# Recurrence: r and k scaled one step further ahead, behind the masking; step 21's logits products behind its bonus products

## The chip, the cores and the metric

One core of one Trainium2 chip. The metric is the device time of one execution in microseconds (us). TensorE is PE in the rows (PEld is its loading of weights), VectorE DVE, ScalarE ACT, GpSimd POOL, SyncE SP. SP only issues DMAs here.

## The reference

Three stages: a linear recurrence with a bonus term, a top-1 mixture of experts, and a second one with soft slots. The change touches the first stage alone.

```python
def _attn_ref(r, k, v, w, u):            # r, k, v: [B=4, H=8, S=768, D=48]
    for t in range(S):
        kt, vt, rt = (k[:, :, t], v[:, :, t], r[:, :, t])
        cur = np.einsum('bhd,bhe->bhde', u[None] * kt, vt)
        y[:, :, t] = np.einsum('bhd,bhde->bhe', rt, state + cur)
        state = w[None, :, :, None] * state + np.einsum('bhd,bhe->bhde', kt, vt)

x = y.transpose(0, 2, 1, 3).reshape(B * S, H * D)      # 3072 x 384
# first mixture, for rows with x @ w_skip > 0:  e = argmax(x @ w_gate)
#     x += prob[e] * relu(x @ w1[e]) @ w2[e]             8 experts, F = 1024
# second mixture: logits = x @ phi (32 slots), softmax over rows gives the slots' inputs,
#     each expert runs its 4 slots, softmax over slots combines them -> out 3072 x 384
```

## The kernel before

**The recurrence in steps.** The sequence is cut into 6 chunks of 128 and there are 4 batches: 24 steps, step j being chunk c = j // 4 of batch b = j % 4 with all 8 heads. Inside a chunk the recurrence is a masked product (like attention without a softmax): r and k are scaled by powers of the decay w, `sc` = k.r, masked below the diagonal, the bonus (u.k.r) put on the diagonal, and the result multiplied with v; what came before the chunk enters through a state `sp`.

**The order** is that of the program: the schedule is manual, each engine executes its instructions as the loop over i writes them. A step i is software-pipelined:

- `load(i+3)` (L510): SP issues the DMA of r and k (`rkb`, L514) and of k and v (`kvt`, L519). A DMA into a buffer waits until the last reader of what lay in it is done; SP issues in order, so what is behind a waiting DMA waits too.
- `scores(i)` (L646): PE makes `sc` (L656) from the scaled `rks` of step i; ACT copies the two blocks that need no mask (`later`, L710); then PE does step i-1's products of r with the state (`inter`, L734) and the first half of its products with v (`av(i-1, 0)`, L753). Then comes a call `between()`, and behind it the bonus products (L666), from `pd` = r*k into the PSUM tile `ud`, which ACT copies to `dts` (L668).
- `trx(i-2)` transposes y of step i-2 (L764, ACT L765).
- `prep(i+1)` (L630): DVE multiplies r and k of step i+1 with decay powers (L635, L636) into `rks`, one of three buffers; POOL makes `pd` (L638). `prepk` makes `kt` on POOL (L644).
- `upd(i)` (L679, PE), `bonus(i)` (L682, PE transposes `dts` back), `moved(i)` (ACT L695), `av(i-1, 1)` (PE, second half, then ACT copies y, L758).
- `past(i)` (L705, DVE) multiplies `sc` with the mask into `at`. The PSUM tile `sc` has one buffer, so `sc` of step i+1 on PE waits for `past(i)`.
- `amask(i)` (L714, DVE) writes the diagonal of `at` from the transposed bonus; `av(i, 0)` on PE waits for it.

**The routing of the first mixture** is threaded through the same steps, per chunk: `route1` (L828: the logits products `lgt`, L837 on PE, copied by ACT, L838) in the steps with i % 4 == 2, and in `between` of steps 21 and 23 for the last groups; `route2` (PE transposes `lgs`, L865), `route2b` (L876, small DVE operations L882 to L901), `route3` (PE), `gates`, `places` and `count` (DVE), `route4` (L952: POOL L956, DVE L957, L958) and `hots` (L798, DVE or POOL). `gathered` (L804) are PE products of these lists. `stored` (L809) writes four finished tiles of x to DRAM in steps 9, 13, 17, ...; `wload` (L963) starts the loads of the first experts' weights in steps 20 to 22, behind the loads of the recurrence.

**Behind the recurrence** come the rest of the routing, the gather of the experts' rows (L1197 on POOL) and the two mixtures.

The change touches `NRK` (number of `rkb` buffers), `load`, `prep` and the loop.

Of the kernel before, what the change touches and what calls it, by code (L numbers as in the profile page):

```python
# [8 lines left out]
F32 = mybir.dt.float32  # L9
# [10 lines left out]
P = 128  # L20
NC_ = S // P
NT = B * NC_
DM = H * D
# [7 lines left out]
PR = 112  # L31
# [443 lines left out]
def tile_main(ctx, tc, rk, kv, wu, wcat, phi, w1, w2, v1, v2, r_in, k_in, v_in, w_in, u_in, wcn, out, dbg=None, force=False):  # L475
    nc = tc.nc
# [8 lines left out]
    wk = ap.enter_context(tc.tile_pool(name="wk", bufs=2))  # L485
# [4 lines left out]
    PE_, DVE_, ACT_, POOL_, SP_ = (mybir.EngineType.PE, mybir.EngineType.DVE, mybir.EngineType.Activation, mybir.EngineType.Pool, mybir.EngineType.SP)  # L490
    mst = ExitStack()
    mst.enter_context(tc.manual_schedule(engines={PE_, DVE_, ACT_, POOL_, SP_}))
    NRK = 5
    ones = fp.tile([P, P], BF16, name="ones")
    nc.vector.memset(ones, float(E))

    def warm(n, w=P):

        wp = ps.tile([P, 2, 4 * P], F32, tag="y", name="wp")[:, 0, 0 : 4 * w]
        for _ in range(n):  # L500
            nc.tensor.matmul(wp, ones, ones[:, 0:w].rearrange("p (o n) -> p o n", o=1).to_broadcast([P, 4, w]), start=True, stop=True)  # L501
# [6 lines left out]
    T = {}  # L508

    def load(j, first=True, last=True):  # L510
        c, b = divmod(j, B)
        if first:
            t = T[j] = {"rk": rkb[j % NRK]}
            nc.sync.dma_start(out=t["rk"], in_=rk[c, b])  # L514
        if not last:
            return
        t = T[j]
        t["kv"] = wk.tile([P, 2, DM], F32, tag="kvt", bufs=5, name=f"kvt{j}")
        nc.sync.dma_start(out=t["kv"], in_=kv[c, b])  # L519

    load(0, last=False)
# [81 lines left out]
    prt = psc.tile([PR, 4, P], F32, name="prt")  # L603
    nc.vector.tensor_mul(prt, pt[:, :, 0:P], iw.to_broadcast([PR, 4, P]))
    pkt = prt[:, :, ::-1]
# [21 lines left out]

    yts = {}

    def prep(j):  # L630
        t = T[j]
        rkt = t["rk"]
        rks = wk.tile([PR, 2, 4, P], F32, tag="rks", bufs=3, name=f"rks{j}")
        t["rs"], t["ks"] = rks[:, 0], rks[:, 1]
        nc.vector.tensor_mul(rks[:, 0], rkt[:, 0], prt)  # L635
        nc.vector.tensor_mul(rks[:, 1], rkt[:, 1], pkt)  # L636
        t["pd"] = wk.tile([PR, 4, P], F32, tag="pd", name=f"pd{j}")
        nc.gpsimd.tensor_mul(t["pd"], rkt[:, 0], rkt[:, 1])  # L638

# [63 lines left out]
    def past(j):  # L703
        t = T[j]
        nc.vector.tensor_mul(t["at"][:, :, 0:4], t["sc"][:, :, 0:4], mh.rearrange("s (a o t) -> s a o t", a=1, o=1).to_broadcast([P, 2, 4, HT]))  # L705
# [122 lines left out]
    def route1(g, pool=ps, tag="r"):  # L828
        c, (j0, nb) = g, GR[g]
        r = RT[c] = {}  # L830
        lgt = pool.tile([P, nb * P], F32, tag=tag, name=f"lgt{c}")
        r["lgs"] = ry.tile([P, nb * P], F32, tag="lgs", bufs=2, name=f"lgs{c}")
        yt, b0 = yts[j0 // B], j0 % B
        for q in range(2):
            for s2 in range(2):
                p = 2 * s2 + q
                nc.tensor.matmul(lgt[64 * s2 : 64 * s2 + 64, :], wcs[:, p, :], yt[:, p, b0 : b0 + nb, :].rearrange("d b t -> d (b t)"), start=(q == 0), stop=(q == 1))  # L837
        nc.scalar.copy(r["lgs"], lgt)  # L838
# [184 lines left out]
    if True:  # L1023
        for i in range(NT):
            if i + 3 < NT:
                load(i + 3)
            rc, rb = divmod(i - 5, B)
            rok = 0 <= rc < NC_ - 1
            if i == 0:
                decays()  # L1030
                warm(5, 48)
                prep(0)
                prepk(0)
                for hf in range(2):
                    r0 = 64 * hf
                    nc.vector.tensor_copy(usel[r0 : r0 + D, :, hf : hf + 1], wt[r0 : r0 + D, 1, :].rearrange("p (a o) -> p a o", o=1))
            scores(i, lambda: route1(i // 2 - 6) if i in (21, 23) else None)
            if i > 1:
                trx(i - 2)
            if rok and rb == 3 or i == 22:  # L1040
                route3(rc, place=T[i]["rp"])
            if rok and rb == 2 and rc < 4:
                route2(rc)
            if i == 21:
                route2(4)
            if i == 23:
                route2(5)
            if rok and rb == 1 and rc < 4:
                route1(rc)
            if i == 0:  # L1050
                prep(1)
                prepk(1)
                for ts in spf:
                    for t in ts:
                        nc.gpsimd.memset(t[:, 4 * D :], 0.0)
            elif i + 1 < NT:
                prep(i + 1)
                prepk(i + 1)
            if i > 0:
                state(i - 1)  # L1060
            upd(i)
            if i == 22:
                c4pt = ps.tile([P, P], F32, tag="r", name="c4pt")
                nc.tensor.transpose(c4pt, c4t.rearrange("p q s -> p (q s)"), ident)
            bonus(i)
            moved(i)
            if i > 0:
                av(i - 1, 1)
            if i in (13, 17, 21, 22):
                gathered(len(LI))  # L1070
            past(i)
            if i == 22:
                nc.vector.tensor_reduce(mcs[:, 0:1], c4pt, axis=AX.X, op=ALU.max)
                dgt = rt.tile([32, 32], F32, tag="dg", bufs=1, name="dgt")
                nc.vector.tensor_scalar(dgt, ident[0:32, 0:32], mcs[0:32, 0:1], None, op0=ALU.mult)
                amask(22)
                weave("pgpgg", g=gates(4), p=places(4))
                tokens(4, nc.gpsimd)
                hots(4, range(4), nc.gpsimd)
            decayed(i)  # L1080
            if i == 21:
                nc.vector.tensor_reduce(cmax, cmg.rearrange("t g s -> t s g"), axis=AX.X, op=ALU.max)
                c4t = fourfold(nc, "t", rt, cmax)
                amask(21)
                route2b(4)
            elif rb == 0 and 1 <= rc < 4:
                route4(rc - 1)
            if i % B and 9 <= i < 22:
                hots(i // B - 2, (i % B,) if i < 20 else (2, 3), nc.vector if i < 20 else nc.gpsimd)
            if i not in (21, 22):  # L1090
                amask(i)
            if rok and rb == 2 and rc < 4:
                route2b(rc)
            if rok and rb == 3:
                weave("gpgpg", g=gates(rc), p=places(rc))
                count(rc)
                tokens(rc, nc.gpsimd)
                hots(rc, (0,) if rc < 3 else (0, 1), nc.vector if rc < 3 else nc.gpsimd)
                if rc == 3:
                    route4(3)  # L1100
            if i == 8:
                wok = rt.tile([PR, 2, 4], F32, tag="wok", bufs=1, name="wok")
                nc.vector.tensor_scalar(wok[:, 0], wt[:, 0, :], WLO, None, op0=ALU.is_ge)
                nc.vector.tensor_scalar(wok[:, 1], wt[:, 0, :], WHI, None, op0=ALU.is_le)
                wmn = mk.tile([PR, 1], BF16, name="wmn")
                nc.vector.tensor_reduce(wmn, wok, axis=AX.XY, op=ALU.min)
            if 20 <= i < 23:
                wload(i - 20)
            if i % B == 1 and 9 <= i < 25:
                stored(i - 9, B)  # L1110
            if i == 22:
                stored(16, B)
            if 3 <= i < 7:
                constants(i)
            if i == 4:
                odd = rt.tile([P, NT], F32, tag="odd", bufs=1, name="odd")
                nc.vector.tensor_reduce(odd[:, 0:1], ident.rearrange("p (a r) -> p r a", r=2)[:, 1:2], axis=AX.X, op=ALU.add)
                nc.vector.tensor_scalar(odd[:, 1:2], odd[:, 0:1], float(-NT), None, op0=ALU.mult)
                tf = rt.tile([P, 2, NT], F32, tag="tf", bufs=1, name="tf")
                nc.scalar.copy(tf, tj_i)  # L1120
                nc.vector.tensor_scalar(tj[:, 0], tf[:, 0], float(NT), odd[:, 1:2], op0=ALU.mult, op1=ALU.add)
                nc.vector.tensor_sub(tj[:, 1], tf[:, 1], tj[:, 0])
                nc.gpsimd.iota(ipl.bitcast(I32), pattern=[[E, CAP]], base=-NOROW, channel_multiplier=0)
                nc.gpsimd.tensor_copy(ipl, ipl.bitcast(I32))
                for t in tok:
                    nc.gpsimd.memset(t, 0.0)
            if i == 6:
                sf = rt.tile([P, E], F32, tag="sf", bufs=1, name="sf")
                nc.vector.tensor_reduce(sf, ident.rearrange("p (q r s) -> p s q r", q=4, s=E)[:, :, :, 0:2], axis=AX.XY, op=ALU.add)
                nc.scalar.copy(selb, sf)  # L1130
# [224 lines left out]
    if True:  # L1355
# [4 lines left out]
        for n in range(NS + 1):  # L1360
# [12 lines left out]
            f = e - 1  # L1373
# [300 lines left out]
```

## Time and profile before

| | us |
|---|---|
| median of 3 runs | 350.14 |
| lowest and highest run | 348.92, 354.14 |
| the profiled execution | 348.07 |
| its span, first to last instruction | 346.3 |
| outside the span | 1.77 |

The profile is of one execution. The span falls into a start (to 8 us), the recurrence (8 to 125), the rest of the routing (125 to 140), the first mixture (140 to 299) and the second (299 to 346). Busy time is time in which an engine executes; "issue" in a row means that an engine stood idle and waited for nothing that the profile shows; PEclk is the clock that TensorE was granted, as a share of full speed.

### The profile page before, as it was taken

The numbers are of one execution on the slowest core, as the hardware profiler recorded it, in microseconds if no ns is written. First come the engines' busy times: TensorE is split into PE (matmuls) and PEld (weight loads), VectorE is DVE, ScalarE is ACT, GpSimd is POOL, SyncE is SP. The second block draws the span as 40 slices with busy tenths as digits, with TensorE's granted clock in tenths as the row PEclk, the third lists the DMA queues.
The fourth block names the chain that finished last, engine by engine and source line by source line (L and its number), as shares of the span: only waits on it lengthen the run. The fifth ranks groups of instructions, "written<-read, shape, count | busy, mean of one in ns | idle before, by whom it ended". The sixth has DMA issues, their size and how long they took to land.

```text
span 346.3 us, 10440 instructions
## 1 busy us (share of the span) xinstructions
PE 321.4 (93%) x4326; PEld 263.9 (76%) x4326; DVE 226.1 (65%) x510; ACT 159.5 (46%) x353; POOL 139.8 (40%) x181
## 2 busy tenths in 40 slices
PE   8699998999998999999999999999999999999950
PEld 8477776767775782999999999998999998534540
DVE  6637676896969865776675848575676845226850
ACT  3235454444543463554645546464645543121360
POOL 3939685776844544804324232525224002200000
PEclk9969999999999998999999999999999999899995
DMA  7976667684879944899788787878866749779096
GB/s 233 287 220 190 187 189 255 199 269 141 279 191 310 387 163 158 266 310 315 252 288 303 239 281 255 263 257 296 294 197 215 254 124 377 256 268 324 10 338 210
DMA packets 45735, 85.29 MB, mean 246 GB/s; under 512 B 3838, under 2 KB 26672, under 8 KB 45680
## 3 DMA queue, kind: packets, MB, share of 16 engines
q1 hardware_dynamic: 43024, 80.63, 70.8%
q0 software_dynamic: 2128, 3.74, 3.9%
q8 instruction: 36, 0.59, 0.7%
q10 hardware_dynamic: 528, 0.16, 0.2%
q14 instruction: 19, 0.16, 0.1%
HBM read 74.49 MB, written 10.10 MB: 244 GB/s over the span
## 4 chain that ended last, share of the span: by engine, by line
PE 79%; DVE 12%; issue 3%; ACT 2%; POOL 1%; ACTq 0%; DVEq 0%
PE yp L1291 7%; PE yp L1292 6%; PE yp L1293 6%; PE hp L1266 6%; PE hp L1269 6%; PE hp L1267 6%; PE yp L753 4%; PE ehp L216 4%; PE sc L656 3%; PE lgt L837 3%; PE ud L679 3%; PE trp L764 3%; PE yp L734 2%; PE wp L501 2%; PE ud L666 2%
## 5 line engine op out<-in xcount | busy, mean ns | idle before, releaser
L1266 PE MATMUL hp<-xhl,wa 128*128 128x240 f32 x192 | 46.1, 282 | 0.2 <-issue 0.2
L1291 PE MATMUL yp<-wb,hh 128*128 128x384 f32 x128 | 45.2, 353 | 0.0
L1004 DVE TENSOR_TENSOR wa<-w,wa 128x768 fp32r<-128x768 f32 x32 | 30.5, 955 | 22.4 <-ACT wa L1016 22.3
L1267 PE MATMUL hp<-xhl,wa 128*128 128x240 f32 x192 | 44.6, 275 | 0.0
L1292 PE MATMUL yp<-wb,hh 128*128 128x384 f32 x128 | 43.0, 336 | 0.0
L1293 PE MATMUL yp<-wb,hl 128*128 128x384 f32 x128 | 42.9, 335 | 0.0
L1197 POOL DMA_INDIRECT xg<-x_d,idg x16 | 19.9, 1242 | 51.9 <-DVE x L1299 38.1
L638 POOL TENSOR_TENSOR pd<-rkb 112x512 f32<-112x512 f32 x24 | 31.1, 1295 | 18.6 <-PE ud L666 15.3
L1321 POOL DMA_INDIRECT lt_d<-lsr,ids x16 | 17.7, 1106 | 50.2 <-ACT xhl L1256 28.3
L1266 PEld LDWEIGHTS hp<-xhl,wa 128*128 128x128 f32 x192 | 36.2, 189 | 0.5 <-ACT dsbv L135 0.5
L1267 PEld LDWEIGHTS hp<-xhl,wa 128*128 128x128 f32 x192 | 36.2, 189 | 0.0
L714 DVE COPY_PREDICATED at<-ih,ud 128x512 f32<-128x512 int32 x24 | 17.7, 738 | 26.0 <-ACT us L695 16.5
L1004 DVE TENSOR_TENSOR wb<-w,wb 128x768 fp32r<-128x768 f32 x32 | 30.5, 953 | 2.1 <-ACT wb L1016 1.7
L1016 ACT CAST wb<-w 128x768 fp32r<-128x768 f32 x32 | 26.8, 838 | 9.5 <-PE yp L1293 5.5
L753 PE MATMUL yp<-at,kvt 64*48 64x64 f32 (+3 forms) x800 | 27.7, 250 | 1.0 <-DVE at L714 0.4
L1276 ACT ACTIVATE hh<-hp 128x480 fp32r<-128x480 f32 x32 | 18.3, 572 | 22.2 <-PE hp L1269 20.0
L1277 DVE SCALAR_TENSOR_TENSOR hl<-hp,hh 128x480 fp32r<-128x480 f32 x32 | 20.9, 654 | 9.7 <-ACT hh L1276 9.2
L1016 ACT CAST wa<-w 128x768 fp32r<-128x768 f32 x32 | 26.9, 840 | 0.0
L1291 PEld LDWEIGHTS yp<-wb,hh 128*128 128x128 f32 x128 | 24.0, 188 | 3.6 <-issue 3.5
L1269 PE MATMUL hp<-xhl,wa 128*128 128x240 f32 x192 | 26.7, 275 | 0.0
L656 PE MATMUL sc<-rks 48*64 48x128 f32 (+1 forms) x768 | 22.1, 252 | 4.5 <-DVE at L705 2.3
L753 PEld LDWEIGHTS yp<-at,kvt 64*48 64x48 f32 (+1 forms) x800 | 22.2, 125 | 5.3 <-issue 1.6
(346 smaller groups left out, 697.1 us busy)
## 6 DMA issues: line engine op xcount, KB each, us to landing
w<-in_w_dram SPq DMA_DIRECT2D x32, 768.0 KB
v<-in_v_dram SPq DMA_DIRECT2D x29, 768.0 KB
rkb<-in_rk_dram SPq DMA_DIRECT2D x24, 448.0 KB
kvt<-in_kv_dram SPq DMA_DIRECT2D x24, 384.0 KB
x_d<-x SPq DMA_DIRECT2D x5, 768.0 KB
out_dram<-ob SPq DMA_DIRECT2D x5, 768.0 KB
x<-in_v_dram SPq DMA_DIRECT2D x2, 768.0 KB
x_d<-x SPq DMA_DIRECT2D x2, 384.0 KB
```

The costliest lines, as they stand in the source:

```text
L638: nc.gpsimd.tensor_mul(t["pd"], rkt[:, 0], rkt[:, 1])
L656: nc.tensor.matmul(sc[c0 : c0 + HT, g, blocks(p, z), :], ks[r0 : r0 + D, p, HT * z : HT * z + HT], rs[r0 : r0 + D, p, HT * z :], start=Tru ...
L753: nc.tensor.matmul(d, kvt[s0 : s0 + HT, 1, h * D : h * D + m], w, start=(c == ph == z == 0), stop=(ph == z == 1))
L1004: nc.vector.tensor_sub(lv, sl, hv.bitcast(F32))
L1016: nc.scalar.copy(hv, sl)
L1266: nc.tensor.matmul(hp[:, f, 0:ROOM], hi[:, k, fs], xh[:, k, 0:ROOM], start=(k == 0 and f == 0), stop=False)
L1267: nc.tensor.matmul(hp[:, f, 0:ROOM], lo[:, k, fs], xh[:, k, 0:ROOM], start=False, stop=False)
L1269: nc.tensor.matmul(hp[:, f, 0:ROOM], hi[:, k, fs], xl[:, k, 0:ROOM], start=False, stop=(k == 2 and f == 1))
L1277: nc.vector.scalar_tensor_tensor(l, p, 0.0, h.bitcast(F32), op0=ALU.max, op1=ALU.subtract)
L1291: nc.tensor.matmul(YP[e][bl], hh[:, f, bs], hi[:, f, :], start=st, stop=False)
L1292: nc.tensor.matmul(YP[e][bl], hh[:, f, bs], lo[:, f, :], start=False, stop=False)
L1293: nc.tensor.matmul(YP[e][bl], hlo[:, f, bs], hi[:, f, :], start=False, stop=en)
```

## The change

Five edits: `NRK` 5 to 4; `kvt` 5 to 4 buffers; `rks` 3 to 4 buffers; the two scalings leave `prep` for a function `scaled(j)` of their own, which step i calls for j = i+2 behind `past(i)` (up to step 2 behind `amask(i)`; `scaled(0)` and `scaled(1)` stand in step 0); and `route1(4)` of step 21 leaves `between` for a place behind `scores(21)`, which ends with the bonus products. Since `load(j)` reuses the buffer of step j-4 instead of j-5, `rkb` of step j now waits for the scaling and `pd` of step j-4, and `kvt` of step j for `av(j-4, 1)`.

```diff
-    NRK = 5
+    NRK = 4
...
-        t["kv"] = wk.tile([P, 2, DM], F32, tag="kvt", bufs=5, name=f"kvt{j}")
+        t["kv"] = wk.tile([P, 2, DM], F32, tag="kvt", bufs=4, name=f"kvt{j}")
...
+    def scaled(j):
+        if j >= NT:
+            return
+        t = T[j]
+        rkt = t["rk"]
+        rks = wk.tile([PR, 2, 4, P], F32, tag="rks", bufs=4, name=f"rks{j}")
+        t["rs"], t["ks"] = rks[:, 0], rks[:, 1]
+        nc.vector.tensor_mul(rks[:, 0], rkt[:, 0], prt)
+        nc.vector.tensor_mul(rks[:, 1], rkt[:, 1], pkt)
+
     def prep(j):
         t = T[j]
         rkt = t["rk"]
-        rks = wk.tile([PR, 2, 4, P], F32, tag="rks", bufs=3, name=f"rks{j}")
-        t["rs"], t["ks"] = rks[:, 0], rks[:, 1]
-        nc.vector.tensor_mul(rks[:, 0], rkt[:, 0], prt)
-        nc.vector.tensor_mul(rks[:, 1], rkt[:, 1], pkt)
...
+                scaled(0)
                 prep(0)
...
-            scores(i, lambda: route1(i // 2 - 6) if i in (21, 23) else None)
+            scores(i, lambda: route1(5) if i == 23 else None)
+            if i == 21:
+                route1(4)
...
             if i == 0:
+                scaled(1)
                 prep(1)
...
             past(i)
+            if i > 2:
+                scaled(i + 2)
...
                 amask(i)
+            if i <= 2:
+                scaled(i + 2)
```

What stands on the engines, in the order of the program. Names end in the step's or group's number and a number of the tile; lines behind L627 are six higher in the changed kernel.

DVE in step 8, from the last routing operation of chunk 0 (`oh0`) on, before:

```order
L901 SCALAR_TENSOR_TENSOR oh0_923<-lgp0_873,m20_921 128x32
L635 TENSOR_TENSOR rks9_983<-rkb4_133,prt_212 112x512
L636 TENSOR_TENSOR rks9_983<-rkb4_133,prt_212 112x512
L705 TENSOR_TENSOR at8_945<-sc8_928,mh_192 128x2x256
L714 COPY_PREDICATED at8_945<-ih_193,ud8_964 128x2x256
L925 TENSOR_REDUCE lgp0_873<-ex0_918 128x4
L936 TENSOR_TENSOR r20_1016<-ud8_964,oh0_923 128x32
```

and with the change:

```order
L907 SCALAR_TENSOR_TENSOR oh0_925<-lgp0_875,m20_923 128x32
L711 TENSOR_TENSOR at8_947<-sc8_930,mh_191 128x2x256
L637 TENSOR_TENSOR rks10_1011<-rkb2_131,prt_211 112x512
L638 TENSOR_TENSOR rks10_1011<-rkb2_131,prt_211 112x512
L720 COPY_PREDICATED at8_947<-ih_192,ud8_966 128x2x256
L931 TENSOR_REDUCE lgp0_875<-ex0_920 128x4
L942 TENSOR_TENSOR r20_1018<-ud8_966,oh0_925 128x32
```

The masking of step 8 (`at8` from `sc8`) now stands ahead of two scalings, and these are of step 10 instead of step 9. Between the masking and the diagonal (`at8` from `ud8`) stand the two scalings.

PE in step 21, from the end of `av(20, 0)` on, before:

```order
L753 MATMUL yp20_2222<-at20_2128,kvt20_1817 48x64 x4
L837 MATMUL lgt4_2239<-yt4_1895,wcs_140 64x512 x4
L666 MATMUL ud21_2246<-pd21_2169,usel_142 32x128 x4
L764 MATMUL trp19_2253<-ident_149,yt4_1895 128x112 x4
L865 MATMUL lgp4_2259<-ident_149,lgs4_2240 128x128 x4
L682 MATMUL ud21_2246<-ident_149,dts21_2251 128x128
```

and with the change:

```order
L759 MATMUL yp20_2224<-at20_2130,kvt20_1819 48x64 x4
L672 MATMUL ud21_2241<-pd21_2168,usel_141 32x128 x4
L843 MATMUL lgt4_2248<-yt4_1894,wcs_139 64x512 x4
L770 MATMUL trp19_2255<-ident_148,yt4_1894 128x112 x4
L871 MATMUL lgp4_2261<-ident_148,lgs4_2249 128x128 x4
L688 MATMUL ud21_2241<-ident_148,dts21_2246 128x128
```

The logits products (`lgt4`) and the bonus products (`ud21` from `pd21`) have changed places.

DVE at the end of step 21 and in step 22, before:

```order
L901 SCALAR_TENSOR_TENSOR oh8_242<-t84_2303,m24_2305 128x32
L635 TENSOR_TENSOR rks23_2370<-rkb3_132,prt_212 112x512
L636 TENSOR_TENSOR rks23_2370<-rkb3_132,prt_212 112x512
L705 TENSOR_TENSOR at22_2332<-sc22_2315,mh_192 128x2x256
L1073 TENSOR_REDUCE mcs_239<-c4pt_2375 128x1
L1075 TENSOR_SCALAR dgt_2396<-ident_149,mcs_239 32x32
L714 COPY_PREDICATED at22_2332<-ih_193,ud22_2351 128x2x256
```

and with the change:

```order
L907 SCALAR_TENSOR_TENSOR oh8_241<-t84_2305,m24_2307 128x32
L711 TENSOR_TENSOR at22_2334<-sc22_2317,mh_191 128x2x256
L1085 TENSOR_REDUCE mcs_238<-c4pt_2374 128x1
L1087 TENSOR_SCALAR dgt_2395<-ident_148,mcs_238 32x32
L720 COPY_PREDICATED at22_2334<-ih_192,ud22_2353 128x2x256
```

The two scalings of step 23 have gone from this place, and none stand behind the masking, since there is no step 24.

## Rows read from the trace of the kernel before

**Rows 1.** The page, part 1: busy us, share of the span, instructions

```profile
PE 321.4 (93%) x4326; PEld 263.9 (76%) x4326; DVE 226.1 (65%) x510; ACT 159.5 (46%) x353; POOL 139.8 (40%) x181
```

**Rows 2.** Windows: from:to length, busy PE PEld DVE ACT POOL, PEclk, DMA share, GB/s

```profile
8.00:125.00 117.00, 108.09 (x2635) 82.16 (x2636) 86.03 (x215) 52.86 (x141) 77.00 (x105) 0.97 0.78 242
140.00:299.00 159.00, 159.00 (x1195) 151.39 (x1193) 104.78 (x193) 84.25 (x164) 50.00 (x50) 1.00 0.81 270
```

**Rows 3.** Waits of 8 to 125 us: who waited for what, us, times, longest

```profile
DVE at L714 <- ACT us L695: 16.5, 11, 3.2
...
PE sc L656 <- DVE at L705: 2.3, 5, 0.9
...
PE yp L753 <- DVE at L714: 0.4, 1, 0.4
```

**Rows 4.** Groups by form, 8 to 125 us: busy us, mean ns | idle before

```profile
L636 DVE TENSOR_TENSOR rks<-rkb,prt 112x512 f32<-112x512 f32 x24 | 16.3, 679 | 0.0
```

**Rows 5.** Timeline, steps 8 to 10: start, us, instruction, [idle before]

```profile
49.36 0.90 PE L656 MATMUL sc<-rks 48*64 48x128 f32 x32 [0.19 <-DVE at L705]
...
53.70 0.90 PE L656 MATMUL sc<-rks 48*64 48x128 f32 x32 [0.45 <-DVE at L705]
...
54.44 0.72 DVE L714 COPY_PREDICATED at<-ih,ud 128x512 f32<-128x512 int32 x1
...
55.49 0.55 PE L734 MATMUL yp<-rks,sp 48*48 48x128 f32 x10 [0.68 <-issue]
```

**Rows 6.** Windows, columns as in rows 2: steps 16 and 17

```profile
89.10:94.80 5.70, 5.35 (x161) 4.30 (x161) 5.57 (x17) 3.11 (x8) 5.29 (x8) 1.00 0.88 290
```

**Rows 7.** Timeline, steps 20 and 21

```profile
108.02 0.90 PE L656 MATMUL sc<-rks 48*64 48x128 f32 x32 [0.88 <-DVE at L705]
108.07 0.74 DVE L714 COPY_PREDICATED at<-ih,ud 128x512 f32<-128x512 int32 x1
...
110.01 1.94 PE L837 MATMUL lgt<-yt,wcs 112*64 112x512 f32 x8 [0.32 <-DVE ltt L957]
...
111.88 0.43 PE L666 MATMUL ud<-pd,usel 112*32 112x128 f32 x8
111.99 0.59 ACT L838 COPY lgs<-lgt 128x512 f32<-128x512 f32 x1 [2.56 <-PE lgt L837]
```

**Rows 8.** Timeline, steps 21 to 23

```profile
114.47 1.26 POOL L638 TENSOR_TENSOR pd<-rkb 112x512 f32<-112x512 f32 x1
114.51 1.25 DVE L889 TENSOR_SCALAR m<-lg 128x4 f32<-128x4 f32 x1
...
117.64 0.29 PE L804 MATMUL lip<-hot,tok 128*32 128x256 bf16 x4
...
117.77 0.68 DVE L705 TENSOR_TENSOR at<-sc,mh 128x512 f32<-128x512 f32 x1
...
118.51 0.90 PE L656 MATMUL sc<-rks 48*64 48x128 f32 x32 [0.58 <-DVE at L705]
```

**Rows 9.** Timeline, step 15: SP's issue of kvt, and DVE

```profile
73.84 0.33 SPq L519 DMA_DIRECT2D kvt<-in_kv_dram  x1
...
82.17 0.69 DVE L705 TENSOR_TENSOR at<-sc,mh 128x512 f32<-128x512 f32 x1
...
84.72 0.74 DVE L714 COPY_PREDICATED at<-ih,ud 128x512 f32<-128x512 int32 x1 [0.74 <-ACT us L695]
```

**Rows 10.** Windows and timeline behind the recurrence: DMA, last store, first gather

```profile
126.00:128.00 2.00, 2.00 (x35) 2.00 (x35) 1.93 (x8) 0.83 (x3) 1.27 (x1) 1.00 0.00 0
...
128.30 0.36 SPq L809 DMA_DIRECT2D x_d<-x  x1
...
133.68 1.28 POOL L1197 DMA_INDIRECT xg<-x_d,idg  x1 [4.46 <-DVE c4v L979]
```

**Rows 11.** Timeline and windows, step 2: an idle of PE and the slow clock

```profile
17.30 1.01 PE L656 MATMUL sc<-rks 48*64 48x64 f32 x19 [2.22 <-issue]
...
16.40:23.40 7.00, 6.10 (x109) 5.01 (x112) 1.84 (x4) 1.92 (x5) 2.51 (x3) 0.51 0.82 222
```

## The prediction

> **What bounds the kernel now.** I read the page's busy times first: PE 321.4 us, 93% of the span, DVE 65%, the others less [rows 1]. So the time is PE's busy time and PE's gaps. The windows by stage say where gaps are: in the first mixture PE is busy for all 159.00 us at full clock, in the recurrence for 108.09 of 117.00 [rows 2]. The change lies in the recurrence. What PE saves there moves everything behind it forward, since the stage that follows is PE's.
>
> The waits of the recurrence name the gap that the change is made for: PE's products `sc` waited five times for the masking L705, 2.3 us together and 0.9 at most; `av` waited once for the diagonal L714, 0.4 us [rows 3]. 2.3 us is therefore the most that the move of the scalings can give directly, 0.7% of the time. The same view shows what covers the move: DVE stood idle ahead of L714 for 16.5 us in 11 steps, waiting for ACT's copy [rows 3]. A scaling is 679 ns, two are 1.36 us [rows 4]; in most steps they can slide into that idle time.
>
> **The scalings, step by step.** No instruction is added or removed. Between two diagonals there stand two scalings before and after, so where DVE has no idle time the diagonals come no sooner; only the masking does, by up to 1.36 us. What is late next is then the diagonal, for which `av` waits.
>
> *Steps 8 to 10.* `sc` waited 0.19 at 49.36 and 0.45 at 53.70. The second gain meets the diagonal: L714 of step 9 ends at 54.44 + 0.72 = 55.16, `av(9, 0)` follows the ten products that began at 55.49, and these had an idle of 0.68 ahead of them that the profile puts down to nothing ("issue") [rows 5]. If this idle keeps its place in time, the 0.45 is swallowed; if it moves along, all 0.64 is won. 0 to 0.64; I take 0.5, since the two waits are real and the diagonal alone leaves room for them.
>
> *Steps 16 and 17.* The fifth wait is the remainder, 2.3 - 0.19 - 0.45 - 0.88 - 0.58 = 0.2. DVE is busy for 5.57 of the 5.70 us from one diagonal to behind the next [rows 6], so the diagonal of step 17 comes no sooner, and `av`'s wait of 0.4 there [rows 3] grows by what `sc` saves. 0 to 0.2; I take 0.
>
> *Steps 20 and 21.* `sc(21)` waited 0.88. Without that PE reaches `av(20, 0)` sooner and stands before the diagonal, which ends at 108.07 + 0.74 = 108.81; then it stands before the logits products, which began at 110.01 when L957 on DVE let go of their PSUM buffer (0.32 of waiting) [rows 7]. L957 stands behind the diagonal and moves no sooner. So the 0.88 ends in two other waits. **The move of `route1(4)`** is to fill the second: the bonus products, 0.43 us, now run ahead of the logits products instead of behind them. But the transposes of `lgs` need ACT's copy, 0.59 us, begun when the logits products ended (111.99) [rows 7]; before, the bonus products and the transposes of x lay under this copy, now the transposes of x alone. The logits products still begin at 110.01, and the copy still ends at 112.6. 0 to 0.43; I take 0.1. The cover is thin: without any work under it, the copy would cost its 0.59.
>
> *Steps 22 and 23.* `sc(23)` waited 0.58: PE was done with its work at 117.64 + 0.29 = 117.93 and went on at 118.51, when the masking begun at 117.77 had ended [rows 8]. Here two scalings leave DVE's queue for good (there is no step 24), so the masking ends 1.36 us sooner, at 117.1, before PE asks, and the diagonal behind it too. All 0.58 is won.
>
> Step 23 and the steps that no wait names: 0. **The third and fourth buffers**: `rks` needs a fourth, since a scaling now comes before the last reader of the oldest is done; it costs no time. The loads come one step later, which is 117 / 24 = 4.9 us [rows 2]: priced below.
>
> **The loads.** The tightest place is where the store of four x tiles stands between them. For step 15: `kvt` was issued at 73.84 [rows 9], and with four buffers this is when the previous step's `kvt`, the 768 KB store and `rkb(17)` go out. The tiles' shapes give 384 + 768 + 448 KB = 1.64 MB, at the stage's 242 GB/s [rows 2] 6.8 us: `rkb(17)` lands at about 80.6. `scaled(17)` wants it behind `past(15)`, which ended at 82.17 + 0.69 and can be 1.36 sooner, 81.5 [rows 9]. 0.9 us of margin, and DVE idles another 0.74 ahead of the next diagonal. Cost 0; bounds 0 and what the first rival gives. The weights' loads, queued behind, slip by 4.9 us. DMA was empty from 126 to 128, the last store went out at 128.30, and the first gather at 133.68 waited for DVE, not for it [rows 10]: 2.9 us of slip past the empty time and 384 KB at 242 GB/s, 1.6 us, still end at 132.8. I take 0, bounds 0 to 0.5 lost.
>
> **The sum**: 0.5 + 0 + 0.1 + 0.58 = 1.2 us. The profiled execution took 348.07 us, so 346.9. The runs lie above it, the lowest by 0.85, the median by 2.07; I put a median of the changed kernel halfway, 1.4 above: 348.3 us.
>
> **Rivals.**
>
> *Late loads (slower than before), 0.12.* DVE takes its queue in order: behind a scaling that waits for `rkb` stand `hots`, the diagonal and the routing, and PE waits for the diagonal. It happens in steps 11, 15 and 19, behind a store. For: 6.8 us of transfer against a margin of 0.9, and the queues carry other loads. Against: the rate in rows 6 is 290 GB/s, above the mean. It decides when `rkb` lands 0.9 + 0.74 = 1.6 us later than worked out, and turns the sign when three such stalls exceed 1.2 us, 0.4 each, that is 2.0 us late each. At 2.5 us late: 3 x 0.86 = 2.6, less 1.2: 348.07 + 1.4 + 1.4 = 350.9.
>
> *Nothing changes, 0.2.* Every gain but that of step 23 was argued against a diagonal that comes no sooner, or an idle of PE without a named cause. If these swallow all of it: 348.07 + 1.4 = 349.5.
>
> *A small instruction on DVE falls beside POOL, 0.1.* L889 took 1.25 us at 114.51, beside POOL's L638 from 114.47 to 115.73 [rows 8], for a comparison of 128x4 elements. The change shifts DVE against POOL by up to 1.36 us at many places. That L889 gets out from under POOL gives nothing: with the masking of step 22 at 117.1, PE has nothing left to wait for there. That another small instruction in a chain to a diagonal falls under a product costs up to 1.25: 348.3 + 1.25 = 349.5. [...]
>
> *The idle of the start goes, 0.06.* PE stood for 2.22 us in the middle of `sc(2)`, without a named wait, and from 16.40 to 23.40 the granted clock was 0.51, the lower of the two levels, with 6.10 us of PE work in it [rows 11]. The clock fell after that idle. With four buffers instead of five fewer loads are queued when the idle comes. If it went, 2.22 us and up to half of 6.10 us would be won; I take 1.5 of the 3.05: 348.3 - 3.7 = 344.6, at the most 343.0. Against: SP's early loads still fill the queues until about the same time, 0.82 of their share in that window. [...]
>
> **How the numbers follow.** 0.52 for the forecast, the rest as given. The forecast's own range: all five waits and the idle at 55.49 won, 348.07 + 0.85 - 2.3 - 0.68 = 345.9, to nothing won in a median like that of before, 350.1. The late loads reach to 351. I give 345.4 to 351.2, which leaves out the idle of the start and the worst of the late loads, about 0.15. Faster or slower by over 2% (7 us, to 343.1 or from 357.1; about what a measurement of this kernel can tell from no change) are outside nearly every case: 0.03 and 0.02.
>
> **What the changed profile would show.** Right: the waits of `sc` for the masking gone or under 0.5 us; `sc(23)` directly behind the products of `lip`; in step 17 `av`'s wait for the diagonal grown; in step 21 the logits products still held by L957 (now L963), and the transposes of `lgs` right behind ACT's copy. Wrong: DVE waiting for `rkb` ahead of a scaling in steps 11, 15 or 19; a gather that waits for the last store; new "issue" idles of PE at other places that eat the gain; or PE's 2.22 us of step 2 gone.

## The result, and the profile after

Over 20 runs each, the changed kernel took 344.14 us in the median and the kernel before 349.37. The ratio is 0.9894, 95% interval 0.9866 to 0.9922: 3.7 us faster, by the interval 2.7 to 4.7. The ratios here and below compare undisturbed executions alone, and not the medians, which here lie 5.2 us apart; the profiles of two experiments, the logits products alone and the first of the scalings alone, are of disturbed executions, whose times are not used below, and one execution of 1025.69 us, of the kernel before with four `kvt` buffers, is left out. The forecast had the direction, and 1.8 us. Against the median that the forecast started from, 350.14, the ratio gives 346.4.

The profiled execution has a span of 341.5 us, 4.8 less than the one before. Its busy times, in the page's first part, are nearly those of before [rows 1]; only the gaps are fewer:

```profile
PE 319.9 (94%) x4326; PEld 262.8 (77%) x4326; DVE 226.2 (66%) x510; ACT 159.8 (47%) x353; POOL 140.6 (41%) x181
```

The windows of the same two stages as in [rows 2] (length, busy PE PEld DVE ACT POOL, PEclk, DMA share, GB/s):

```profile
8.00:125.00 117.00, 110.93 (x2675) 84.93 (x2676) 88.62 (x227) 53.78 (x142) 78.19 (x106) 0.97 0.76 241
140.00:299.00 159.00, 158.90 (x1196) 149.76 (x1194) 103.63 (x191) 84.02 (x163) 49.56 (x47) 1.00 0.80 269
```

More work of PE fits into the same 117 us, the last 3 of which now belong to the stage behind, since the recurrence ends sooner; the first mixture is as full as before.

Steps 8 to 10 (timeline, as in [rows 5]). Both products `sc` start without a wait, the idle of 0.68 is gone too, and what PE meets now is the diagonal:

```profile
47.96 0.85 PE L662 MATMUL sc<-rks 48*64 48x128 f32 x32
...
51.88 0.85 PE L662 MATMUL sc<-rks 48*64 48x128 f32 x32
...
53.26 0.72 DVE L720 COPY_PREDICATED at<-ih,ud 128x512 f32<-128x512 int32 x1
...
54.04 0.55 PE L759 MATMUL yp<-at,kvt 64*48 64x128 f32 x16 [0.60 <-DVE at L720]
```

Over the whole recurrence (waits of 8 to 125 us, as in [rows 3]) no wait of `sc` for the masking is left, where there were 2.3 us, and `av`'s waits for the diagonal have grown from 0.4 us to 1.7:

```profile
PE yp L759 <- DVE at L720: 1.7, 4, 0.6
```

Steps 17, and 20 to 23 (as in [rows 6 to 8]): the waits for the diagonal, for L963 (once L957) and for ACT's copy, and `sc(23)` right behind the products of `lip`:

```profile
91.83 0.55 PE L759 MATMUL yp<-at,kvt 64*48 64x128 f32 x16 [0.57 <-DVE at L720]
...
103.94 0.85 PE L662 MATMUL sc<-rks 48*64 48x128 f32 x32
...
105.65 0.55 PE L759 MATMUL yp<-at,kvt 64*48 64x128 f32 x16 [0.15 <-DVE at L720]
106.13 0.42 PE L672 MATMUL ud<-pd,usel 112*32 112x128 f32 x8
...
106.79 1.94 PE L843 MATMUL lgt<-yt,wcs 112*64 112x512 f32 x8 [0.24 <-DVE ltt L963]
...
109.42 0.66 PE L871 MATMUL lgp<-ident,lgs 128*128 128x128 f32 x4 [0.15 <-ACT lgs L844]
...
114.36 0.29 PE L810 MATMUL lip<-hot,tok 128*32 128x256 bf16 x4
...
114.58 0.90 PE L662 MATMUL sc<-rks 48*64 48x128 f32 x32
```

Step 2 (as in [rows 11]): the idle stays, at 2.00 us. The granted clock is 0.50 for 6.8 us in both profiles, but from 17.84 to 24.66 instead of 16.54 to 23.36, so that the window of [rows 11] holds less of it; before, it fell inside the idle, and 0.76 us of the 6.8 were idle, and now it falls behind the idle, and PE is busy throughout. First the timeline, then the windows 16.40 to 23.40 and 19 to 21, then 19 to 21 of the kernel before. The column to look at in the windows is the DMA share, next to last:

```profile
16.98 0.61 PE L662 MATMUL sc<-rks 48*64 48x64 f32 x19 [2.00 <-issue]
```

```profile
16.40:23.40 7.00, 6.42 (x134) 5.34 (x136) 2.64 (x5) 2.26 (x6) 2.27 (x2) 0.60 0.41 122
...
19.00:21.00 2.00, 2.00 (x24) 1.41 (x27) 0.00 (x0) 0.48 (x1) 1.32 (x2) 0.50 0.01 2
```

```profile
19.00:21.00 2.00, 2.00 (x24) 1.34 (x25) 0.55 (x1) 0.65 (x2) 1.20 (x1) 0.50 1.02 277
```

With four buffers the DMA engines have run empty at 19 to 21 us, where with five they were full. This is what the forecast had no term for in its sum.

**Where the 4.8 us of the two profiles lie.** ACT's copies of y (L758 before, L764 after) mark the steps on one clock. Between the copies of the steps named, after against before: to step 3, -1.04; steps 3 to 7, 0; 7 to 10, -0.85; 10 to 13, -1.15; 13 to 16, -0.15; 16 to 19, +0.17; 19 to 21, -0.27; 21 to 23, -0.03; from there to the first product of the first mixture +0.80; that mixture 0; the start of the second -1.69, its rest -0.51. The +0.80 and the -1.69 go with the clock and not with the change. In the stretch of the first the clock was 0.88 before and 0.77 after, and the other profiles, at 0.88 to 1.00, took 12.9 to 14.6 us for it (14.15 before, 14.95 after), old and new code alike. In the window 299 to 304 the clock was 0.66 before and 1.00 after; the start of the second mixture took 13.5 us before and 11.8 after, and 13.3 to 15.0 in the other profiles, again with old and new code alike (14.9 in a second profile of the changed kernel). The change's own part in this pair of profiles is the 3.3 us up to step 23.

### The profile page after: what moved, and what is told of

It reads as the page before. It is cut to its first block, busy times and chain, and to the rows that moved or that the text cites. A ratio compares the mean times of both kernels' runs of the same rounds, so it can differ in the third digit from the quotient of the medians.

```text
span 341.5 us, 10444 instructions
## 1 busy us (share of the span) xinstructions
PE 319.9 (94%) x4326; PEld 262.8 (77%) x4326; DVE 226.2 (66%) x510; ACT 159.8 (47%) x353; POOL 140.6 (41%) x181
## 4 chain that ended last, share of the span: by engine, by line
PE 73%; DVE 13%; DMA 4%; issue 2%; ACT 2%; POOL 1%; SPq 0%; ACTq 0%; POOLq 0%
PE yp L1305 7%; PE yp L1306 7%; PE yp L1307 7%; PE hp L1280 6%; PE hp L1283 6%; PE hp L1281 6%; PE yp L759 3%; PE ehp L216 3%; PE lgt L843 3%; PE sc L662 2%; PE trp L770 2%; PE ud L685 2%; DVE at L720 2%; DMA x_d<-x 2%; PE dpst L129 2%
## 5 line engine op out<-in xcount | busy, mean ns | idle before, releaser
L759 PE MATMUL yp<-at,kvt 64*48 64x64 f32 (+3 forms) x800 | 27.0, 250 | 1.9 <-DVE at L720 1.7
L1305 PEld LDWEIGHTS yp<-wb,hh 128*128 128x128 f32 x128 | 24.0, 188 | 3.5 <-issue 3.5
L759 PEld LDWEIGHTS yp<-at,kvt 64*48 64x48 f32 (+1 forms) x800 | 21.7, 125 | 6.4 <-DVE at L720 2.7
L1306 PEld LDWEIGHTS yp<-wb,hh 128*128 128x128 f32 x128 | 24.1, 188 | 0.0
```

Source lines behind the costliest of these rows:

```text
L759: nc.tensor.matmul(d, kvt[s0 : s0 + HT, 1, h * D : h * D + m], w, start=(c == ph == z == 0), stop=(ph == z == 1))
L1305: nc.tensor.matmul(YP[e][bl], hh[:, f, bs], hi[:, f, :], start=st, stop=False)
L1306: nc.tensor.matmul(YP[e][bl], hh[:, f, bs], lo[:, f, :], start=False, stop=False)
```

## The experiments

Theory Q: what stands in the DMA queues holds back the fetch of PE's instructions; PE's idles with "issue" as cause, and what the clock does behind them, are this; fewer buffers keep fewer loads queued. In the two profiles packets of 16 KB stand on the instruction queue, one for every 256 of PE's records from the 449th on; a crossing is a place where PE goes on to the next 256. Theory S, the rival: the move of the scalings gave everything, and the idles went because the program shifted. The late loads remained as a third. The runs of a group stood on one chip with the kernel before.

**The buffers alone.**

```diff
-    NRK = 5
+    NRK = 4
...
-        ... tag="kvt", bufs=5 ...
+        ... tag="kvt", bufs=4 ...
```

> Only the buffers of the loads go from 5 to 4 (rkb and kvt); the scalings and the logits products stay where they were. Theory Q (fewer loads stand in the DMA queues, so PE's idles that no wait explains, 2.22 us in step 2 and 0.32 + 0.68 + 0.34 + 0.68 = 2.02 us in steps 3 to 13, shrink): those of steps 3 to 13 fall below 0.7 us together, the waits of sc for the masking stay near 2.3 us, the time falls by 1 to 2 us (ratio 0.994 to 0.997). Theory S (the move of the scalings gave everything, the idles went because the program shifted): idles of at least 1.5 us stay, ratio 0.998 to 1.002. Late loads (the buffers cost): DVE waits for rkb, ratio above 1.002.

Ratio 0.9918 (0.9885 to 0.9952), 2.9 us. Waits of the recurrence (us, times, longest): `sc`'s for the masking are all there.

```profile
PE sc L656 <- issue: 2.6, 1, 2.6
...
PE sc L656 <- DVE at L705: 2.3, 5, 0.9
PE yp L734 <- issue: 1.2, 1, 1.2
```

So by this run most of the gain comes without moving one instruction. The idles fell less than theory Q had it: one of 1.20 at 61.84 stood in place of 2.02 in four pieces.

**The scalings alone**, with five buffers for both loads and three for `rks`:

```diff
+    def scaled(j):
...
             past(i)
+            if i > 2:
+                scaled(i + 2)
```

> Only the scalings move; five buffers for rkb and kvt as before, three for the scaled r and k, logits products of step 21 in the old place. Theory Q: the waits of sc for the masking fall from 2.3 us to under 0.5, the unexplained idles of steps 3 to 13 stay near 2 us, 1.2 us are won: ratio 0.995 to 0.998. Theory S: waits gone and idles gone too, ratio 0.988 to 0.992, as with the whole change.

Ratio 0.9902 (0.9857 to 0.9948), as much as the whole change. This spoke for theory S. Repeated in a later group:

> The move of the scalings alone again, on the chip of the other three, since its first interval (0.986 to 0.995) does not fit the whole change with five kvt buffers (0.995 to 1.006). Theory Q: 0.995 to 0.999, an idle of 0.3 to 3 us in step 3. Rival (the move carries the gain by itself): 0.988 to 0.993.

Ratio 1.0000 (0.9959 to 1.0041). The two intervals of this one kernel do not meet, so the ratio of a single group says less than its interval does. What the profile of the second run shows is clear, though: no wait of `sc` for the masking is left, and two idles stand behind step 2, in steps 3 and 12:

```profile
17.27 0.70 PE L662 MATMUL sc<-rks 48*64 48x64 f32 x19 [2.28 <-issue]
...
24.33 0.79 PE L759 MATMUL yp<-at,kvt 64*64 64x128 f32 x10 [1.13 <-issue]
...
68.64 0.31 PE L759 MATMUL yp<-at,kvt 64*48 64x64 f32 x3 [0.80 <-issue]
```

**The logits products alone.**

```diff
-            scores(i, lambda: route1(i // 2 - 6) if i in (21, 23) else None)
+            scores(i, lambda: route1(5) if i == 23 else None)
+            if i == 21:
+                route1(4)
```

> Only the logits products of step 21 go behind the bonus products. Both theories: at most 0.3 us won, ratio 0.998 to 1.001; the logits products still begin when L957 has ended, the transposes of lgs wait 0.1 to 0.3 us for ACT's copy. A rival in which this edit carries the surplus: ratio below 0.997.

Ratio 0.9960 (0.9905 to 1.0015): nothing that can be told from no change, though the 0.9960 itself lies where the rival had put it; the next run speaks against the rival. In its profile `lgp` waited for ACT's copy, as in the changed kernel (0.15 in both).

**The whole change without them.**

> The whole change without the move of the logits products. Both theories: within 0.4 us of the whole change, ratio 0.988 to 0.992; the logits products wait for L957 some 0.4 us longer than the 0.24 us of the changed kernel. If this edit carries the surplus: ratio 0.994 or more.

Ratio 0.9877 (0.9824 to 0.9931). The logits products waited 0.59 for L963 instead of 0.24. From step 19 to 21 this kernel took 10.37 us, the changed one 10.30, the one before 10.57: 0.07 for the edit. With five `kvt` buffers it was 10.37 without the edit (the scalings alone, repeated) and 10.40 with it (the next run), so a gain of the edit is not shown.

**Which buffer.** The whole change, with `kvt` at five:

> The whole change, but five buffers for kvt (four for rkb). SP issues in order, and kvt(4) no longer waits for av(0,1): it and rkb(5) go out some 7 us sooner, before 10 us. Theory Q (what stands in the DMA queues holds back the fetch of PE's instructions): the idle behind step 2 comes back, at the crossing in step 3 (0.3 to 3 us, as in the three profiles with five buffers), idles of steps 4 to 13 partly; 1 to 2.5 us slower than the whole change, ratio to before 0.993 to 0.998. Rival (which buffers does not matter, the crossings fell elsewhere): no idle in step 3, ratio 0.987 to 0.992.

Ratio 1.0004 (0.9949 to 1.0060): one buffer more for `kvt`, and the gain is gone, more of it than theory Q had said. In the profile the idle of step 2 grew to 3.27 and the DMA engines were full again from 19 to 21 us; the idle in step 3 that was expected did not come.

```profile
18.29 0.61 PE L662 MATMUL sc<-rks 48*64 48x64 f32 x19 [3.27 <-issue]
```

```profile
19.00:21.00 2.00, 2.00 (x27) 1.28 (x19) 0.69 (x1) 0.64 (x2) 0.64 (x1) 0.50 1.03 253
```

With `rkb` at five instead:

> The whole change, but five buffers for rkb (four for kvt). In SP's order kvt(j) now waits longest, so one load of rkb more is queued at the start, nothing else. Theory Q: like the whole change within 0.5 us, ratio 0.987 to 0.992, no idle in step 3. Rival (rkb's buffer is the one that counts): an idle of 0.3 to 3 us in step 3, ratio 0.993 or more.

Ratio 0.9908 (0.9852 to 0.9965), as the whole change. This run and the one before it stood on one chip and differ in which load has the fifth buffer; their intervals share only 0.9949 to 0.9965. And the kernel before with nothing but four `kvt` buffers:

> The kernel before with four buffers for kvt and nothing else changed (rkb keeps five). Theory Q with kvt as the one that counts in SP's order: the queues run empty between 19 and 23 us, the lag of the instruction packet behind PE's entry in step 2 falls from 4.4 us to 1.5 to 2.5, no idle of 0.3 to 3 us in step 3, the waits of sc for the masking stay at 2.3 us: ratio 0.990 to 0.996, as with both buffers (0.992). Rival (the move of the scalings carries the gain): 0.998 to 1.002.

Ratio 0.9949 (0.9896 to 1.0002), inside what theory Q gave and just short of being told from 1. DMA engines empty at 19 to 21 us, waits for the masking untouched, no idle in step 3:

```profile
PE sc L656 <- issue: 2.3, 1, 2.3
PE sc L656 <- DVE at L705: 2.3, 5, 0.9
```

```profile
19.00:21.00 2.00, 2.00 (x25) 1.41 (x26) 0.03 (x1) 0.48 (x1) 1.30 (x2) 0.50 0.17 45
```

**One load more.** A load of 384 KB that nobody reads, behind `kvt(3)`:

```diff
+            if i == 0:
+                spare_kv = kp.tile([P, 2, DM], F32, name="spare_kv")
+                nc.sync.dma_start(out=spare_kv, in_=kv[5, 3])
```

> The whole change plus one load of 384 KB in step 0 into a buffer that nobody reads, behind kvt(3). Theory Q: the queues hold 1.2 to 1.6 us more work before 16 us; the idle of step 2 or the one in step 3 grows by about that, 1 to 3 us slower than the whole change, ratio 0.991 to 0.998. Rival (idles don't depend on the queues): idles as in the changed kernel, ratio 0.987 to 0.992.

Ratio 0.9931 (0.9880 to 0.9982), which is not apart from the whole change's. The idle of step 2 was 2.00 as before and none came in step 3. Behind PE's next crossing the packet of instructions began at 19.46 instead of 18.50, so it was held back by about 1 us, but early enough to cost no idle. Theory Q's size failed here: one load more at that place is not enough.

**A later load at the start.** The load of step 3 was to wait for step 1's buffer. In the first try it stood in the program ahead of step 1's own reads, so step 1 waited for it and was computed from the r and k of step 3:

```diff
-            t = T[j] = {"rk": rkb[j % NRK]}
+            t = T[j] = {"rk": rkb[j if j < 3 else (1, 0, 3, 2)[(j - 3) % 4]]}
```

> The whole change; only the load of rkb(3) takes the buffer of step 1 instead of a fresh one, so that it, and kvt(3) behind it on SP, are issued at about 10.5 us instead of 4.7 and 5.6 (the queues still have work until 12 us). Theory Q: fewer loads stand ahead when PE enters the 256 instructions before the idle (9.75 us), so the instruction packet that began at 14.16 begins at 11.5 to 13 us, the idle of 2.00 us in step 2 falls below 1 us, and the stretch of half clock behind it gets shorter or goes: 1 to 4 us faster than the whole change, ratio 0.978 to 0.987. Rival (the packet begins at a fixed time or by PE's progress): 14 us and 2 us of idle as before, ratio 0.987 to 0.992. If the loads come too late: DVE waits for rkb ahead of scaled(3), ratio above 0.99.

Ratio 1.0041 (0.9991 to 1.0091), DVE waiting 5.8 us for `rkb` in one place: it says nothing on the theories. With the load behind step 1's reads, and the line above as it is:

```diff
-            if i + 3 < NT:
+            if 0 < i < NT - 3:
                 load(i + 3)
...
                 prep(1)
+                load(3)
                 prepk(1)
```

> The whole change; the load of rkb(3) takes the buffer of step 1 and stands in the program behind the scaling and the bonus factor of step 1 (in the run before this one it stood ahead of them, so that step 1 waited for it and read it). SP issues it at about 10.5 us instead of 4.7, kvt(3) behind it; the queues have work until 12 us. Theory Q: fewer loads stand ahead of the instruction packet that began at 14.16 in the changed kernel; it begins at 11.5 to 13.3, the idle of 2.00 us in step 2 falls below 1 us and the clock does not fall behind it; PE enters the instructions of step 3 that it entered at 23.07 before 22 us: 1 to 4 us faster than the whole change. Rival (the packet begins at a fixed time or by PE's progress): 14 us and 2 us of idle as before, the same time as the whole change.

Ratio 0.9900 (0.9844 to 0.9955), no faster than the changed kernel beside it (0.9897), where theory Q had 1 to 4 us. Its mechanism did show. The packet of instructions began at 11.67 instead of 14.16, and the idle of step 2 was gone altogether. The part of the DMA queues that carries instructions, windows 11.6 to 12.8 of this kernel (packets, MB, share):

```profile
q8 instruction: 1, 0.02, 5.5%
```

The changed kernel has no such packet in that window. At 11 to 12 and 12 to 13 us the DMA share was 0.76 and 0.12 with the load held back, 1.11 and 1.02 in the changed kernel. PE itself came to the 256 records before that idle later than in the changed kernel, at 10.95 us instead of 9.75, so the packet does not follow PE's progress alone; by these shares it was the queued loads that held it. Why the time did not fall is seen in this profile alone: PE waited for `kt` of step 0, which POOL began 1.7 us later than in the changed kernel, held by the load of `kvt(0)` (2.80 us of waiting for it, against 1.14). The clock, which was not to fall, was at 0.50 from 12.9 us on, behind that wait, for 6.8 us, and still in the window 17 to 19:

```profile
PE ud L685 <- POOL kt L650: 1.6, 1, 1.6
```

```profile
17.00:19.00 2.00, 2.00 (x63) 2.00 (x57) 1.84 (x3) 0.84 (x2) 1.62 (x2) 0.50 0.59 146
```

From the copy of step 0 to that of step 3 it took 11.83 us, the changed kernel 15.39; up to step 0 it took 17.46 against 14.73. Whether the late first `kvt` belongs to this edit or to this run stays open: `kvt(0)` is issued at the same place in both, and over the other profiles POOL began that instruction anywhere between 8.21 and 9.28 us, here at 9.89.

**The changed kernel again**, in one group with the later load, four `kvt` buffers alone and the scalings again:

> The changed kernel again, to stand beside the other three on one chip: ratio 0.986 to 0.993. Theory Q: no idle without a named wait in step 3, 1.5 to 2.8 us of it in step 2.

Ratio 0.9897 (0.9856 to 0.9939). The idle of step 2 was 2.03.

**The stretches of all these profiles**, in us, between ACT's copies of y in the steps named (those of the two later loads are left out, since they shift the start):

| kernel | kvt buffers | scalings | to 3 | 7-10 | 10-13 | 13-16 | 19-21 | 21-23 |
|---|---|---|---|---|---|---|---|---|
| before | 5 | old | 31.16 | 15.61 | 15.60 | 12.58 | 10.57 | 7.59 |
| scalings alone, again | 5 | new | 33.40 | 14.75 | 15.33 | 12.43 | 10.37 | 6.95 |
| change, kvt 5 | 5 | new | 31.93 | 14.75 | 14.40 | 12.42 | 10.40 | 6.95 |
| buffers alone | 4 | old | 30.71 | 16.39 | 14.41 | 12.57 | 10.57 | 7.60 |
| kvt 4 alone | 4 | old | 30.41 | 14.88 | 14.55 | 12.83 | 10.56 | 7.60 |
| the change | 4 | new | 30.12 | 14.76 | 14.45 | 12.43 | 10.30 | 7.56 |
| the change again | 4 | new | 28.99 | 14.90 | 14.46 | 12.43 | 10.29 | 6.95 |
| without logits' move | 4 | new | 31.42 | 15.04 | 14.43 | 12.43 | 10.37 | 7.13 |
| change, rkb 5 | 4 | new | 28.51 | 14.74 | 14.42 | 12.42 | 10.38 | 7.21 |
| one load more | 4 | new | 30.21 | 15.06 | 14.88 | 12.43 | 10.31 | 7.28 |

The columns split the change. "To 3" goes by the buffers of `kvt`: 32.2 in the mean of three with five, 30.1 in the mean of seven with four, 2.1 us. But the two sets meet (31.16 at the least with five, 31.42 at the most with four), and about half of the 2.1 goes with the lower clock: behind the idle of step 2 it held for 6.8 us in seven of the ten profiles, for 3.4 in the change again, not at all with `rkb` at five, and for 3.4 and again 6.8 behind the idle of step 3 in the scalings alone. Among the seven the means are 31.5 and 30.6. The last three go by the place of the scalings: 12.57 to 12.83 with the old, 12.42 or 12.43 with the new; 10.56 or 10.57, and 10.29 to 10.40; 7.59 or 7.60, and 6.95 to 7.28, or 7.56 in the changed kernel's first profile, where an idle of 0.29 stands. What makes 6.95 in some and 7.28 in others, where PE has no idle at all, is not known. 10 to 13 is 14.4 to 14.6 wherever neither a packet of instructions nor a load was late.

**That the idles are PE's instruction fetch** can be read from the same ten profiles, beyond what the theories asked. Count PE's records in order of time: its products, its weight loads and its waits for semaphores. From step 2 to the end of the recurrence the ten have 21 idles of PE over 0.2 us with "issue" as cause; each comes after 449 records or a multiple of 256 more (within one record), in old and new code alike, and each ends 1.30 to 1.69 us behind the end of one packet of 16 KB on the instruction queue. At none of the 200 places of this kind does PE go on sooner than 1.26 us behind the end of the packet whose turn it is. So an idle is what a late packet leaves uncovered, and a shift of the program does not make it. For the place in step 3 (705 records) the packet began 4.1 to 4.4 us after PE had gone on at 449 in the three profiles with five `kvt` buffers, 1.5 to 2.2 in six with four, and 2.5 with the load more. With `kvt` at five it was as late as before, 4.1 us; no idle came, since PE, at the lower clock, reached that place only at 25.24 us, 1.5 behind the packet, instead of 24.38 before. The packet of step 3 in the DMA view of the kernel before, window 21.7 to 22.9, and of the changed one, window 18.4 to 19.7 (packets, MB, share):

```profile
q8 instruction: 1, 0.02, 6.0%
...
q8 instruction: 1, 0.02, 5.5%
```

## Why the prediction was right, and where it was wrong

**The scalings: right, 0.8 to 1.0 of 1.2 us.** *Steps 8 to 10*: of the range 0 to 0.64 I took 0.5; it was about 0.1 (14.88 with the old scalings and four `kvt` buffers, 14.76 with the new). The two waits went, and the diagonal took back 0.60. What I called the lower end, "the diagonal comes no sooner", was nearly the whole answer; the idle of 0.68 went, but for another reason. *Steps 16 and 17*: 0 was right: 0.15 won before the diagonal, and `av`'s wait for it grew from 0.40 to 0.57. *Steps 20 and 21*: 0.2 to 0.27 in place of 0.1, of which the logits' move has 0.08 at most; the logits products still began only when L963 let them, and the transposes of `lgs` waited 0.15 for ACT's copy. *Steps 22 and 23*: 0.65 in place of 0.58 in the three profiles with 6.95, 0.45 in the mean of the seven with the new scalings, and 0.03 in the pair of the result, where the idle of 0.29 fell there. Together 0.1 + 0 + 0.27 + 0.65 = 1.0, or 0.8 with the means. The waits of the result's pair say the same: 2.3 us for the masking gone, 1.3 more for the diagonal.

**The loads: wrong, and this is the other 2 to 3 us.** The step that failed is "The loads. ... Cost 0; bounds 0 and what the first rival gives". I priced one buffer less only as loads that come later, a loss or nothing. It has a gain: what is not queued does not stand ahead of PE's instructions (DMA share at 19 to 21 us: 0.01 instead of 1.02). With four buffers for `kvt` alone the runs gave 1.8 us (0.9949, not quite told from nothing), with both 2.9 (0.9918), with both and the scalings 3.7; and five `kvt` buffers under the whole change gave 0. That the time still fell into the stated range is luck: its lower end was made of five waits and one idle wholly won, and what moved the time there was a term that stood at nothing.

**The rival of the start was the right mechanism at the wrong instruction.** I asked whether the idle of 2.22 us in step 2 would go, saw that the early loads would still fill the queues until then, and gave it 0.06. The idle did stay (2.00). (The clock fell at 16.54, inside that idle from 15.08 to 17.30, and not after it, as I read.) But `kvt(4)` and `rkb(5)` now go out at 15 us and not at 7 and 8, so the queues run empty when the packet of the next crossing, in step 3, is due; the packet that began 4.4 us behind PE began 1.5 us behind it. The stretch at the lower clock was as long as before in this pair, 6.8 us, and shorter in two other profiles with four `kvt` buffers. I looked for the effect on one idle and not on the ones that follow it, though the 0.32, 0.34 and 0.68 were in the trace.

**Late loads**: they came, mostly at other places than forecast, and the price was small. DVE waited for `rkb` in no step of the changed kernel's first profile and for 0.9 us in two of its second; with a load more for 1.82 us in step 11, a place that was named, and 0.67 in step 21; without the logits' move four times, 2.4 us together, most of it in steps 1 and 2. That one was none the slower (0.9877); the load more took 0.4 us longer in steps 10 to 13 (14.88 against 14.46). The cover in front of the diagonal held.

**The last store**: 0 was right. The first gather waits for DVE as before [rows 10]:

```profile
130.29 1.28 POOL L1211 DMA_INDIRECT xg<-x_d,idg  x1 [4.39 <-DVE ltt L1220]
```

**The small instruction beside POOL**: L889, now L895, stands beside POOL's product (111.17 to 112.45 us) as before and costs about as much, 1.19 us against 1.25 [rows 8]; nothing hung on it. The scalings kept their 679 ns [rows 4], also in their new place.

```profile
111.30 1.19 DVE L895 TENSOR_SCALAR m<-lg 128x4 f32<-128x4 f32 x1
```

**The sum's last step**: halfway between 0.85 and 2.07 is 1.46, not 1.4; it moves nothing.

**What stays open.** The scalings alone gave 0.990 once and 1.000 once; by the stretches they are worth 0.8 to 1.0 us, 0.997 to 0.998, between the two. Apart from that 0.990, the kernels with five `kvt` buffers lie at 0.996 to 1.000 and those with four at 0.988 to 0.995, so the split of the 3.7 us between loads and scalings is known to about 1 us and no better. Half of the gain up to step 3 goes with how long the lower clock held, and why it held for 6.8, 3.4 or 0 us behind nearly the same idle the runs do not show.

## What to carry to other kernels

A deeper load buffer is not free where it only queues earlier (here a fifth `kvt` buffer took the whole change from 0.9894 to 1.0004): ask what else goes through the DMA engines at that time, here PE's own instructions. An idle of PE with "issue" as its only cause, at a place where the DMA share is 1, is a question to put to the queues: does it end just behind a packet of the instruction queue (here 1.30 to 1.69 us behind it)? Its size changes from run to run: of the two profiles of the changed kernel one had 0.29 us of it in steps 21 to 23, the other none. Where a masking is freed from work ahead of it, look for the next wait of the same consumer on the same engine: here it took back 0.60 of 0.64 us in one place and nothing in another, where the work had left the queue for good.

## What the runs showed of the hardware

- PE's instructions come as packets through the DMA engines, 16 KB for 256 records here, and one starts late while loads are queued: 4.1 to 4.4 us behind PE at the place in step 3 with a DMA share of 1.02 to 1.05 at 19 to 21 us, 1.5 to 2.5 us with 0.01 to 0.82 there. With the load of step 3 held back, the packet before it began at 11.67 us instead of 14.16, and PE's idle of 2.00 us went. At the crossing in step 2 PE's idle was 1.45 to 3.27 us in ten profiles, with loads queued, and none with a load held back.
- The clock does not follow the length of the idle alone: behind 2.00 us of it, in one profile of the changed kernel, the granted clock was 0.50 of full speed for 6.8 us, behind 2.03 us, in the other, for 3.4 us. Behind 1.45 us, with `rkb` at five, it stayed at 1.00 through the whole window in which the kernel before had 0.51:

```profile
16.40:23.40 7.00, 5.77 (x160) 4.67 (x161) 4.57 (x8) 2.88 (x9) 3.62 (x4) 1.00 0.57 194
```

That profile's span was 340.6 us, the shortest of all.
